# A long convolution as two blocks of 1024 with 1024-point transforms, in place of one 2048-point transform, beside a Fourier-mixing matmul

## The chip, the core and the metric

The kernel runs on one core of a Trainium2 chip. The metric is the device time of one execution in microseconds. Before the change the median of three runs is 596.75 us (596.72 to 599.88).

## What is computed

Two independent results are joined side by side. Part A multiplies a 2048 x 512 input by Fourier matrices on both sides and keeps the real part. Part B is a convolution of 2048 samples in each of 512 channels. Its kernel K is first built from 128 complex exponentials per channel.

```python
a = jnp.einsum("bsd,ed->bse", x, dft_hid_re)
b = jnp.einsum("bsd,ed->bse", x, dft_hid_im)
yA = jnp.einsum("ts,bse->bte", dft_seq_re, a) - jnp.einsum("ts,bse->bte", dft_seq_im, b)
...
K = 2.0 * jnp.einsum("dn,dnl->dl", C, P).real     # P = exp(A dt * position)
y = jnp.fft.irfft(jnp.fft.rfft(u_t, L2) * jnp.fft.rfft(K, L2)[None], L2)[:, :, :L]   # L2 = 2 L = 4096
yB = y.transpose(0, 2, 1) + u * D_skip
```

## The kernel before, in words

**The order of the work** is fixed when the program is built. A planner (`Plan`, line 71) runs every piece of work as a generator that names the engine it needs and an assumed duration. `run` (line 129) always takes the piece that can start first, and among equals the one with the lowest urgency number. The instructions of each engine come out in that order, and on the chip each engine follows its list strictly and waits where an operand isn't there. All DMAs but two are issued by one queue, SP.

**Part A** (class `Fnet`) is the filler. Its matmuls, line 299, have the highest urgency number, 5, so they go wherever TensorE has nothing else. There are 1920 of them, three for each product of a 128 x 128 by a 128 x 512 block. For them ScalarE and VectorE split each fp32 block that moves through the array into two halves, "hi" (line 184) and "lo" (line 186). One split serves twelve matmuls, and at most three splits are held ahead. The first stage's result goes to DRAM and is read back (lines 318 and 270). The last results leave by line 321.

**Part B** (class `Ssm`) goes through these steps.

- The input's first transform stage, `stage1_u` (line 788): 8 steps, each with matmuls (line 798), four evictions (line 808) and two stores to `xu` in DRAM (line 814).
- The tables of exponentials, in 16 chunks of 32 channels: `seed_args` and `seeds` (lines 560 to 606), `tables1` (line 640) and `tables2` (line 660). They are mostly VectorE work on lines 529, 538, 552 and 558, with squares on ScalarE (line 545). `tables2` has one buffer, so that a chunk's table can be started only when the previous one has been used.
- `taps` (line 707): 16 times 64 small matmuls (line 725), which turn a chunk's tables into samples of K. Two chunks make a group, for which `stage1_k` (line 743) does the kernel's first transform stage (line 755), and stores it to `xk` (line 769).
- The products, by four channel quarters h and four frequency groups q (`product`, line 865). Both spectra are loaded (line 849), the second transform stage runs on TensorE (line 876, 64 matmuls), ScalarE copies it out of PSUM (line 889), VectorE multiplies (lines 892, 894, 902, 905), TensorE does the first inverse stage (line 912), ScalarE copies it out (line 927), and it goes to `zs` in DRAM (line 933). Quarter h can start when its two kernel groups are stored, so the products of quarters 0 to 2 fall into the time of the tables and those of quarter 3 come after the last taps.
- The last inverse stage (`inverse`, line 948): `zs` is read back (line 954), 16 matmuls for each half quarter (line 959), and the output leaves by lines 975, 978 and 964 to 971.

Two PSUM buffers, f0 and f1, serve all of part B (`banks`, line 401). VectorE and ScalarE take part in both A and B.

The before form of the convolution is one transform of 2048 points at the frequencies k + 1/4, whose real part gives the 2048 wanted samples. A product is therefore one complex multiplication per frequency.

## Time and profile before

| What | Value |
|---|---|
| Median of three runs | 596.75 us |
| The profiled execution | 596.03 us |
| Its span, first to last instruction | 594.2 us |
| TensorE busy | 583.7 us (98%) |
| VectorE busy | 496.2 us (84%) |
| ScalarE busy | 380.7 us (64%) |
| DMA, mean | 212 GB/s, 125.97 MB |

The profile's page lists busy time per engine, the span in 40 slices, the chain of work that ended last, and groups of instructions by line. PE is TensorE, DVE VectorE, ACT ScalarE, SP the engine that issues the DMAs. A group's mean duration includes the time in which an instruction overlaps its neighbour, so the sum over a group can be larger than the engine's busy time. The timeline gives starts, from which the real spacing is read. 1.8 us of the execution lie outside the span.

### The profile page before, as it was taken

The page shows a single profiled execution, that of the slowest core. Times are in us where ns is not written, and L with a number is a line of the kernel's source. Part 1 is how long each engine was busy: PE and PEld are TensorE (multiplying, and loading weights), DVE is VectorE, ACT ScalarE, POOL GpSimd, SP SyncE. Part 2 cuts the span into 40 slices and gives each one's busy share as a digit, 9 for nine tenths or more (in the row PEclk, how much of TensorE's full clock was granted, in tenths as well). Part 3 has the DMA queues.
Part 4 walks back from the last instruction along what each step waited for, and adds up shares of the span by engine and source line. Part 5 has one row for each costly group of instructions (what it writes and reads, how often), then busy time and mean ns, then how long its engine had stood idle before and what let it go on. Part 6 is the DMA issues. An engine that isn't in the chain of part 4 may idle for free.

```text
span 594.2 us, 16953 instructions
## 1 busy us (share of the span) xinstructions
PE 583.7 (98%) x6982; PEld 451.0 (76%) x6982; DVE 496.2 (84%) x883; ACT 380.7 (64%) x745; POOL 4.7 (1%) x12
## 2 busy tenths in 40 slices
PE   7999999999999999999899999999999999999997
PEld 5866668778788777877687788778877877887775
DVE  6985989999999999999999999999999954255410
ACT  4689984856676767758574976677764635264532
POOL 0000000000000000000000000000000000000000
PEclk8999999999999999999999999999999999999999
DMA  8999996263394268546857793459798734998674
GB/s 270 295 334 362 310 362 202 77 208 94 98 267 126 90 183 252 144 136 157 251 179 207 200 256 131 140 154 278 234 276 225 241 114 145 287 358 258 186 248 143
DMA packets 141150, 125.97 MB, mean 212 GB/s; under 512 B 46224, under 2 KB 106128, under 8 KB 140816
## 3 DMA queue, kind: packets, MB, share of 16 engines
q1 hardware_dynamic: 140656, 124.49, 68.8%
q8 instruction: 55, 0.90, 0.6%
q10 hardware_dynamic: 416, 0.39, 0.2%
q14 instruction: 23, 0.19, 0.1%
HBM read 82.12 MB, written 42.73 MB: 210 GB/s over the span
## 4 chain that ended last, share of the span: by engine, by line
PE 82%; DVE 7%; ACT 6%; issue 2%; DMA 2%; SPq 0%; ACTq 0%; DVEq 0%
PE acc L299 64%; PE f L876 5%; PE f L725 5%; PE f L912 3%; PE f L959 3%; DVE prod L529 2%; PE f L755 2%; DVE lo L186 2%; DVE t L538 2%; ACT hi L184 1%; DMA uk<-in_x 1%; ACT L586 1%; DMA raw<-in_sT 1%; DMA xu<-z 1%; ACT seed L574 1%
## 5 line engine op out<-in xcount | busy, mean ns | idle before, releaser
L299 PE MATMUL acc<-hi,x_hi 128*128 128x512 f32 x640 | 257.8, 403 | 2.9 <-ACT x_hi L184 1.5
L299 PE MATMUL acc<-lo,x_hi 128*128 128x512 f32 x640 | 250.5, 391 | 0.1
L299 PE MATMUL acc<-hi,x_lo 128*128 128x512 f32 x640 | 250.4, 391 | 0.1
L529 DVE TENSOR_TENSOR prod<-t,cs 128x1024 f32<-128x1024 f32 (+4 forms) x192 | 163.3, 869 | 3.6 <-ACT t L667 1.4
L186 DVE TENSOR_TENSOR lo<-raw,hi 128x512 fp32r<-128x512 f32 x160 | 109.1, 686 | 63.9 <-ACT hi L184 63.9
L184 ACT ACTIVATE hi<-raw 128x512 fp32r<-128x512 f32 x160 | 100.3, 629 | 92.7 <-PE acc L299 72.8
L299 PEld LDWEIGHTS acc<-hi,x_hi 128*128 128x128 f32 x640 | 120.6, 188 | 48.4 <-issue 20.5
L299 PEld LDWEIGHTS acc<-hi,x_lo 128*128 128x128 f32 x640 | 120.6, 188 | 26.5 <-DVE x_lo L186 0.5
L299 PEld LDWEIGHTS acc<-lo,x_hi 128*128 128x128 f32 x640 | 120.7, 189 | 24.0 <-DVE lo L186 0.9
L538 DVE TENSOR_TENSOR t<-prod 128x512 f32<-128x512 f32 (+4 forms) x192 | 94.4, 511 | 1.1
L545 ACT ACTIVATE square<-t 128x256 f32<-128x256 f32 (+1 forms) x64 | 36.6, 572 | 22.9 <-DVE t L538 21.2
L313 ACT ACTIVATE y<-acc 128x512 f32<-128x512 f32 x48 | 28.4, 596 | 14.7 <-PE acc L299 12.8
L889 ACT ACTIVATE uk<-f 128x1024 f32<-128x1024 f32 x32 | 32.1, 1016 | 6.3 <-PE f L876 5.1
L725 PEld LDWEIGHTS f<-t,t 128*32 128x32 f32 x2048 | 29.5, 110 | 7.0 <-issue 4.3
L725 PE MATMUL f<-t,t 128*32 128x64 f32 x2048 | 32.2, 220 | 0.8 <-issue 0.8
L892 DVE TENSOR_TENSOR z<-uk 128x512 f32<-128x512 f32 x32 | 21.9, 686 | 8.4 <-ACT uk L889 7.6
L558 DVE TENSOR_TENSOR t<-square 128x128 f32<-128x128 f32 (+1 forms) x64 | 24.6, 384 | 0.3 <-ACT square L545 0.3
L927 ACT ACTIVATE z<-f 128x512 f32<-128x512 f32 x32 | 17.6, 596 | 10.9 <-PE f L725 5.8
L876 PE MATMUL f<-xt_k,w 64*32 64x128 f32 x1024 | 22.8, 271 | 1.0 <-issue 1.0
L604 ACT ACTIVATE cs<-cs 128x352 f32<-128x352 f32 x32 | 15.9, 537 | 12.1 <-DVE cs L599 12.1
L894 DVE TENSOR_TENSOR uk<-uk 128x512 f32<-128x512 f32 x32 | 22.1, 689 | 0.8
L552 DVE SCALAR_TENSOR_TENSOR t<-t 128x128 f32<-128x128 f32 (+2 forms) x48 | 22.3, 465 | 0.4
(85 smaller groups left out, 440.6 us busy)
## 6 DMA issues: line engine op xcount, KB each, us to landing
raw<-in_sT SPq DMA_DIRECT2D x127, 256.0 KB, 3.4
p<-y SPq DMA_DIRECT2D x32, 256.0 KB, 4.1
xt_u<-xu SPq DMA_DIRECT2D x32, 256.0 KB, 4.4
xk<-xk_sb SPq DMA_DIRECT2D x32, 256.0 KB, 4.0
xt_k<-xk SPq DMA_DIRECT2D x32, 256.0 KB, 5.1
zs<-z SPq DMA_DIRECT2D x32, 256.0 KB, 3.7
zl<-zs SPq DMA_DIRECT2D x16, 512.0 KB, 6.1
raw<-p SPq DMA_DIRECT2D x32, 256.0 KB, 3.8
```

Of the source, the lines that this page charges most:

```text
L184: self.nc.scalar.activation(hi, src, AF.Copy)
L186: self.nc.vector.tensor_tensor(lo, src, hi.bitcast(F32), op=OP.subtract)
L299: nc.tensor.matmul(acc[d], l[:, cols], r, start=k == 0 and n == 0, stop=k == len(items) - 1 and n == 2)
L313: self.nc.scalar.activation(y, ps, AF.Copy, scale=-1.0 if g[2] == 1 else 1.0)
L529: self.nc.vector.tensor_tensor(p.rearrange("p k d c m -> p k (d c) m"), src.rearrange("p d c l -> p (d c) l")[:, None, :, rows].to_broadca ...
L538: self.nc.vector.tensor_tensor(dst[:, :, :, rows], p[:, 0], p[:, 1, :, ::-1], op=OP.add)
L545: self.nc.scalar.activation(sq, t[:, :, :, m // 2:m], AF.Square)
L552: self.nc.vector.scalar_tensor_tensor(t[:, :, 1, m:2 * m:2], t[:, :, 0, m // 2:m], 2.0, t[:, :, 1, m // 2:m], op0=OP.mult, op1=OP.mult)
L558: self.nc.vector.tensor_tensor(t[:, :, 0, m:2 * m:2], box[0][:, :, 0], box[0][:, :, 1], op=OP.subtract)
L725: nc.tensor.matmul(ps[32 * j:32 * j + 32, i], t1[:, d, c], t2[:, d, c], start=c == 0, stop=c == 1, tile_position=(0, 32 * j))
L876: nc.tensor.matmul(got[r][1][32 * xx:32 * xx + 32, g, o:o + PART], self.w2[rows, 2 * q + r, xx, 32 * c:32 * c + 32], xt[rows, r, xx], star ...
L889: a.activation(uk[:, r].rearrange("p g n c d -> p g (n c d)"), p, AF.Copy)
```

## The change

The 2048 samples are cut into two blocks of 1024, and the transforms have 1024 points, at k + 1/4. From the blocks U0, U1 of the input and K0, K1' of the kernel (the first kernel stage's constants add K0 times i to the second block) come two spectra: U0 K0 for the first output block, and U0 K1' + U1 K0 for the second. That is three complex multiplications for two output frequencies, where there were two. The data volume of the spectra stays the same.

- First stages: `f1u` has 32 rows and 64 columns per tile in place of 64 and 128. A step of `stage1_u` has eight matmuls of 512 columns in eight positions of the array, where it had four in two positions.
- Second stage: the same 64 matmuls per product, with the blocks on the two halves of the partitions. The spectra's loads and the stores to `zs` now cover 64 partitions each (two per group, one for each block), where each covered 128.
- The product has ten VectorE operations of 128 x 512 where it had six.
- Last inverse stage: 32 matmuls in eight positions for each half quarter, where there were 16 in two positions. The last quarter is fetched back from `zs` by groups, in eight DMAs of 16 partitions with 16 KB on each, and is evicted by ScalarE and VectorE in two steps at the end. Before, it came in four pieces of 128 partitions.
- Buffers: quarter 3's four input spectra are loaded early, into the buffers of quarters 0 to 2, and its kernel spectra have four buffers. The product has three in the last phase.
- Planner: ScalarE's seeds, squares and table copies get a more urgent number (`URGENT`), an event of the first split is set earlier, and the product waits for the last kernel group.

The core of the diff:

```diff
+URGENT = (lambda: -0.5),
...
-        yield "pe", 1.82
-        for m in range(2):
-            for r in range(2):
-                rows = slice(64 * r, 64 * r + 64)
-                nc.tensor.matmul(got[m][1][:, r], self.f1u[rows], u[rows, m], start=True, stop=True,
-                                 tile_position=(64 * r, 0))
+        yield "pe", 0.95
+        for r in range(4):
+            for h in range(2):
+                rows = slice(32 * r, 32 * r + 32)
+                nc.tensor.matmul(got[r // 2][1][64 * h:64 * h + 64, r % 2], self.f1u[rows], u[rows, h], start=True,
+                                 stop=True, tile_position=(32 * r, 64 * h))
...
-        for r in range(2):
-            self.nc.sync.dma_start(xt[:, r], view[2 * q + r])
+        for g in range(2):
+            self.nc.sync.dma_start(xt[64 * g:64 * g + 64].rearrange("p r x d -> p (r x) d"), view[g, q])
...
-            v.tensor_tensor(P[:, r], t[:, r], u[:, r], op=OP.mult)
-            yield "dve", dve(512), *APART
-            v.tensor_tensor(t[:, r], t[:, r], u[:, r, :, ::-1], op=OP.mult)
...
+            v.tensor_tensor(P[:, r], t[:, r], u[:, r, 0:1].to_broadcast([128, 2, 2, PART]), op=OP.mult)
+        yield "dve", dve(512), *APART
+        v.tensor_tensor(W, t[:, :, 0], u[:, :, 1], op=OP.mult)
+        yield "dve", dve(512)
+        v.tensor_tensor(P[:, :, 1], P[:, :, 1], W, op=OP.add)
+        yield "dve", dve(512), *APART
+        v.tensor_tensor(W, t[:, :, 0], u[:, :, 1, ::-1], op=OP.mult)
+        for r in range(2):
+            yield "dve", dve(512), *APART
+            v.tensor_tensor(t[:, r], t[:, r], u[:, r, 0:1, ::-1].to_broadcast([128, 2, 2, PART]), op=OP.mult)
...
         v.tensor_tensor(u[:, :, :, 0], P[:, :, :, 0], P[:, :, :, 1], op=OP.subtract)
         self.plan.put(b.zbs)
         yield "dve", dve(512), *APART
+        v.tensor_tensor(t[:, :, 1], t[:, :, 1], W, op=OP.add)
+        yield "dve", dve(512)
         v.tensor_tensor(t[:, :, :, 0], t[:, :, :, 0], t[:, :, :, 1], op=OP.add)
...
+    def fetch_last(self, z, q, left):
+        yield "dma", load(512), *URGENT
+        for g in range(2):
+            self.nc.sync.dma_start(z[64 * g + 16 * q:64 * g + 16 * q + 16],
+                                   self.zs[3][g, 8 * q:8 * q + 8].rearrange("s c l d -> (s c) l d"))
...
-        yield "pe", 0.1 + 0.1025 * n
-        for w in range(n // 2):
-            for y in range(2):
-                nc.tensor.matmul(ps[64 * y:64 * y + 64, w // 4, PART * (w % 4):PART * (w % 4) + PART],
-                                 self.ib[:, n * i + 2 * w + y], z[:, 2 * w + y], start=True, stop=True,
-                                 tile_position=(0, 64 * y))
+        yield "pe", 0.95
+        for w in range(m):
+            for j in range(4):
+                for g in range(2):
+                    rows, l = slice(64 * g, 64 * g + 64), 4 * w + j
+                    nc.tensor.matmul(ps[32 * j:32 * j + 32, g, PART * w:PART * w + PART], self.ib[rows, n * i + l],
+                                     z[rows, l], start=True, stop=True, tile_position=(64 * g, 32 * j))
...
+        if h == 3:
+            yield "act", act(512)
+            nc.scalar.activation(*part(0), AF.Copy)
+            yield "dve", dve(512)
+            nc.vector.tensor_copy(*part(1))
+            self.give(k)
+            for g, queue in enumerate((nc.sync, nc.scalar if i else nc.sync)):
+                queue.dma_start(y[:, g], part(g)[0])
```

## The prediction

> **What bounds the kernel now.** I read the busy shares first, then the stages, the chain, the groups of instructions and the timeline. The page's slices:

> ```profile
> PE   7999999999999999999899999999999999999997
> ...
> DVE  6985989999999999999999999999999954255410
> ACT  4689984856676767758574976677764635264532
> ```

> TensorE is full from end to end. VectorE is just as full until the last table is done at 481.7 us, and half idle afterwards. The stages, cut at the first matmuls and at that moment (columns: start:end, length, then busy us of PE, PEld, DVE, ACT, POOL; clock, DMA share, GB/s), and two pieces of interest:

> ```profile
> 8.25:481.69 473.44, 470.77 (x5533) 365.04 (x5534) 454.68 (x817) 327.93 (x662) 4.28 (x7) 1.00 0.69 209
> 481.69:594.20 112.51, 107.80 (x1439) 83.11 (x1437) 37.99 (x57) 48.05 (x77) 0.24 (x1) 0.99 0.73 223
> ...
> 40.00:52.00 12.00, 12.00 (x52) 7.98 (x52) 3.62 (x7) 11.89 (x26) 0.00 (x0) 1.00 0.98 351
> ...
> 500.00:550.00 50.00, 50.00 (x702) 39.14 (x701) 21.25 (x32) 23.51 (x38) 0.00 (x0) 1.00 0.95 284
> ```

> So two engines bound the first 482 us together, and TensorE alone the rest. The chain (start, length, piece) shows TensorE's pieces and, at the end, its cover:

> ```profile
> 482.09 1.05 PE f L912 x32
> 483.14 1.90 PE f L725 x122
> ...
> 548.33 1.05 PE f L912 x32
> ...
> 554.97 1.96 PE f L876 x128
> ...
> 563.29 1.05 PE f L912 x32
> 564.34 12.47 PE acc L299 x54
> 576.81 1.02 PE f L959 x16
> ...
> 580.65 1.90 PE f L959 x32
> 582.55 7.76 PE acc L299 x33
> ```

> The reader is to see the length of each kind of burst, and that 54 matmuls of part A (12.5 us) stand between the last L912 and the first L959 that needs its result. A run of n L299 costs 0.2266 n + 0.25 us (x12 2.97, x102 23.36 in the same chain).

> **TensorE's work.** A first-stage step is 1.92 us (L798 x8), eight of them. The new one has 16 executions of 512 columns in eight array positions; L912 has 32 of 256 in eight positions of the same 32*64 shape, as many columns, and takes 1.05. Saved: 8 x 0.87 = 7.0. A half quarter of the last stage is 1.90 (L959 x32); the new one has half the columns of L876 (1.96, eight positions of 64*32), so 0.98. Saved: 8 x 0.92 = 7.4. Part B interrupts L299 60 times, not 62: 0.5. If TensorE alone counted, the span would be 594.2 - 14.9 = 579.3. If the positions didn't overlap the gain is 0 at worst; neither row leaves room for much under half.

> **VectorE's work.** A product has ten operations for six. L892 to L905 are 0.60 us apart where the next doesn't need the last one's result, 0.73 where it does; the mean sum of the six is 3.85. Broadcast operands cost nothing (L529 with them 685 ns at 512 columns, L892 686). Ten with three or four dependent neighbours: 10 x 0.60 + 3.5 x 0.12 = 6.4. Added: 2.6 a product, 41 us in all. On average 496 + 41 fits into 579. It doesn't fit where it falls: in the compiled order, 11 of the 16 products stand ahead of the last table.

> **When the last taps (L725) can start.** The order of the instructions gives what stands ahead of them.
> - TensorE: 1725 L299 in place of 1587 (+138 x 0.2266 = 31.3), one more second stage (1.96), two more interruptions (0.5), less 7.0 for the first stage and four half quarters (3.7): 483.1 + 23.1 = 506.2.
> - VectorE: 11 x 2.6 = 28.6 and 11 more splits at 0.60 (6.6): 483.1 + 35.2 = 518.3.

> VectorE is the later one. But it was idle before 130 us for 17.5 us, of which 8.4 lie in 40 to 52, where ScalarE was full (row above) with seeds, table loads and evictions of the first stage. In the new order the first-stage steps come further apart (after 96, 135, 183 matmuls of part A; before after 102, 120, 135), and seeds are more urgent. I take those 8.4 as recovered: 518.3 - 8.4, **510**. Ends: 506.2 and 518.3. VectorE waiting means that TensorE waits at the next taps, since its order is fixed.

> **From there to the end.** Before: 594.2 - 483.1 = 111.1. Off go 138 L299 (31.3), the second stage (1.96), four half quarters (3.7) and four interruptions (1.0): 73.1. Then comes a new wait. After the last L912 only 27 L299 are left (6.4 us), then the last L959. Between them lie eviction, store to zs and fetch. Before, L912 ended at 564.34, the fetch was issued at 570.33 (6.0), and fetches landed after 5.6 us: 11.6 in all, hidden under 12.5. Now 11.6 - 6.4 = 5.2 us are bare (ends 3.5 and 8). Nothing is queued behind the waiting L959 but the end. It ends with an eviction and an output DMA (out_yb 2.6 us to landing, out_ya 2.3) with one more eviction in series (at most 0.69): 0.7 later than before (3.9).

> 510 + 73.1 + 5.2 + 0.7 = 589.0 span; the execution has 1.8 us outside it (596.03 - 594.2): **591**. The median of 596.75 lies 0.7 above the profiled execution; half a per cent of it, about what this measurement can tell from no change, is 593.8 to 599.7.

> TensorE's clock: the first L299 ran at 0.246 us each (x97 in 23.90), later 0.2266; an idle of 2 us near 290 left it at 1.00. [...]

> **Costed at nothing:** ScalarE's new priorities and early loads of quarter 3's input spectra (ScalarE is 64% busy, and the early loads lie where DMA's share is 0.63, between 103 and 482); smaller constants. If the early loads were late they would cost TensorE a product's loading, about 5 us.

> **Rivals.**
> 1. *VectorE recovers more* (the tables keep up with TensorE): 506.2, so 587. Against it: 11 products' additions come into a stretch with 1% idle.
> 2. *VectorE recovers nothing*: 518.3, so 599. For it: ScalarE's number of instructions is unchanged (749 to 747), so its backlog may only move.
> 3. *The SP queue becomes the bound of the tail* (slower). After the last kernel group (about 6 us after the last taps) the order has 67 transfers' worth of 256 KB, 17.6 MB. At 500 to 550 us a share of 0.95 moved 284 GB/s, so one costs 0.88 us of the queue and all 59, in 73 us: 14 us of slack. 30 of them now touch only 64 or 16 partitions (8 spectrum loads of the kernel and 4 of the input, 10 stores, 8 fetches). No row shows such a transfer. Between "as a wide one" (0) and "twice" (30 x 0.88 = 26 more) I take 0 for the forecast, the nearest rows being wide ones of the same bytes; it decides from 1.5 times on. At twice: 26 - 14 = 12 us, 603. They queue in one line, so the late fetches pay.
> 4. *The array positions don't overlap as in L912 and L876*: 14.4 more, 605. Against it: same shapes in both rows.

> [...]

> **Chances.** Forecast (510, wide-like transfers) 0.37; rival 1 0.10; rival 2 0.17; rival 3 0.32; rival 4 0.04. The forecast's own range is 587 to 596 (its waits' ends); rival 3 from 595 (half the price) to 605. Eight in ten: from below rival 1, where the bare wait is at its short end, to rival 3: 584 to 604. Faster by over 0.5%: most of the forecast and rival 1, 0.44. Within: rival 2 and the edges, 0.21. Slower: rivals 3 and 4 and a late rival 2, 0.35.

> **What would show it.** First-stage steps of 1.05 and half quarters of about 1.0 us in the chain; products of ten operations, 6.4 us where nothing stands between; the last L725 at 510 (506 rival 1, 518 rival 2), with idle of TensorE ahead of taps; a bare wait of 5 us before the last L959, ended by the fetch from zs. Rival 3: landings of the 64-partition loads and of the fetches well above 5 us, with the DMA share near 1 and L876 or the first L959 waiting for them. I would be wrong if ScalarE, not VectorE, holds the tables, or if evictions that wait for stores stop ScalarE's queue.

## The result, and the profile after

The changed kernel takes 619.86 us (median of six executions, 615.0 to 622.4), the kernel before 596.9 us beside it. The ratio is 1.0363, 95% interval 1.0311 to 1.0415: slower by 3.6%, where 591 us and a range of 584 to 604 had been forecast. The profiled execution takes 622.4 us with a span of 620.6. All executions compared below are undisturbed ones; one of the four of `after_zuk` was in a slower state of the chip and is left out of its median.

The slices of the page after:

```profile
PE   8999999999999989999999998999879999979772
...
DVE  6999989999999998999997998989979999256700
...
PEclk9999999999999999999999999999899999999895
```

TensorE, full to the end before, has a small gap near 220 us, more of them from 370 us on and a thin end. VectorE is full until the last table, which is done at 520.3 us instead of 481.7. The granted clock, at 9 tenths or more before in all slices but the first, has dents at 434 to 450 us, at 574 to 590 and at the end. The same by stages, cut at the last taps, with two pieces of 10 us (columns: start:end, length, busy us of PE, PEld, DVE, ACT, POOL; clock, DMA share, GB/s):

```profile
8.25:521.46 513.21, 499.09 (x6028) 387.31 (x6030) 488.34 (x874) 343.51 (x683) 3.54 (x7) 0.99 0.73 202
521.46:620.60 99.14, 75.15 (x1267) 55.56 (x1267) 42.95 (x67) 33.75 (x53) 0.52 (x1) 0.90 0.88 203
440.00:450.00 10.00, 7.59 (x86) 5.56 (x86) 8.75 (x16) 4.42 (x8) 0.00 (x0) 0.83 0.72 269
550.00:560.00 10.00, 7.22 (x144) 5.45 (x143) 6.72 (x11) 3.65 (x5) 0.00 (x0) 0.83 1.16 238
```

In the last stage the DMA share rises from 0.73 to 0.88 while the rate falls from 223 to 203 GB/s: the engines are busier and move less. TensorE is idle for 24 us of 99. The chain (start, length, piece) names what for:

```profile
457.68 1.92 PE f L735 x126
459.60 3.67 issue
...
521.46 1.93 PE f L735 x128
...
540.15 6.50 DMA xt_k<-xk
...
552.03 2.78 issue
...
574.81 11.76 DMA zl<-zs
...
602.48 9.20 DMA zl<-zs
611.81 3.72 PE f L1018 x126
```

Three things stand here that the chain of before didn't have: loads of spectra and fetches of `zs` for which TensorE waits, "issue" waits of up to 3.67 us in the middle of a burst of matmuls (0.80 in the chain of before), and last matmuls that take 3.72 us where 128 at the full clock take 2.2 (64 take 1.09). The DMA issues of the page (count, KB each, median us from issue to landing) answer to 5.1 for `xt_k` and 3.7 for `zs` before:

```profile
xt_k<-xk SPq DMA_DIRECT2D x32, 256.0 KB, 7.2
zs<-z SPq DMA_DIRECT2D x32, 256.0 KB, 4.4
```

### The profile page after: what moved, and what is told of

Its sections match the earlier page's. It is cut to its first block, busy times and chain, and to the rows that moved or that the text cites. A ratio compares the mean times of both kernels' runs of the same rounds, so it can differ in the third digit from the quotient of the medians.

```text
span 620.6 us, 17639 instructions
## 1 busy us (share of the span) xinstructions
PE 580.5 (94%) x7302; PEld 446.6 (72%) x7302; DVE 534.8 (86%) x948; ACT 381.8 (62%) x743; POOL 4.3 (1%) x12
## 4 chain that ended last, share of the span: by engine, by line
PE 51%; DVE 25%; DMA 12%; issue 6%; ACT 4%; SPq 1%; ACTq 0%; DVEq 0%
PE acc L307 39%; DVE prod L538 7%; DMA zl<-zs 5%; DVE lo L194 5%; DVE t L547 4%; PE f L735 4%; PE f L902 3%; DMA par<-par_dram 2%; DMA xt_k<-xk 2%; PE f L947 2%; PE f L810 1%; PE f L1018 1%; PE f L765 1%; DVE z L924 1%; DMA raw<-in_wT 1%
## 5 line engine op out<-in xcount | busy, mean ns | idle before, releaser
L321 ACT ACTIVATE y<-acc 128x512 f32<-128x512 f32 x48 | 28.6, 596 | 23.2 <-PE acc L307 14.7
L913 ACT ACTIVATE uk<-f 128x1024 f32<-128x1024 f32 x32 | 31.9, 1020 | 12.5 <-PE f L902 12.5
L902 PE MATMUL f<-xt_k,w 64*32 64x128 f32 x1088 | 24.8, 275 | 4.6 <-issue 3.5
L1018 PE MATMUL f<-zl,ib 64*32 64x128 f32 x512 | 12.6, 327 | 15.6 <-DMA zl<-zs 15.6
L962 ACT ACTIVATE z<-f 128x512 f32<-128x512 f32 x32 | 17.5, 588 | 9.5 <-PE f L947 7.2
L1018 PEld LDWEIGHTS f<-zl,ib 64*32 64x32 f32 x512 | 9.1, 125 | 19.5 <-issue 15.7
```

What stands on the lines that cost most here:

```text
L321: self.nc.scalar.activation(y, ps, AF.Copy, scale=-1.0 if g[2] == 1 else 1.0)
L902: nc.tensor.matmul(got[r][1][32 * xx:32 * xx + 32, g, o:o + PART], self.w2[rows, 8 * q + 4 * r + xx, 32 * c:32 * c + 32], xt[rows, r, xx], ...
L913: a.activation(uk[:, r].rearrange("p g n c d -> p g (n c d)"), p, AF.Copy)
L1018: nc.tensor.matmul(ps[32 * j:32 * j + 32, g, PART * w:PART * w + PART], self.ib[rows, n * i + l], z[rows, l], start=True, stop=True, tile_ ...
```

## The experiments

Three theories stood at the start. *Transfers*: loads, stores and fetches that touch 64 or 16 partitions take longer in the one line of the SP queue. *Tables*: VectorE's 44 more operations ahead of the last table hold the taps. *Order*: the new priorities (on ScalarE's work and on a few loads) give a worse order. A fourth, of the instruction blocks, came up on the way.

### Each cause alone, in the kernel before

`before_narrow`: spectra loaded and `zs` stored as two transfers of 64 partitions in place of two of 128, the same bytes.

```diff
-        for r in range(2):
-            self.nc.sync.dma_start(xt[:, r], view[2 * q + r])
+        for g in range(2):
+            self.nc.sync.dma_start(xt[64 * g:64 * g + 64].rearrange("p r x d -> p (r x) d"), view[q, g])
```

> The kernel before, with the spectra's loads and the stores to zs done as two transfers of 64 partitions in place of two of 128: the same bytes and rows of 512 bytes, 96 transfers, and the order of every engine unchanged. Narrow theory (64 partitions are slower to reach than 128): the loads of the kernel's spectra land in about 7 us, not 5, and the kernel is 3 to 10 us slower, most of it after 500 us where the queue was at a share of 0.95. Tables theory (the added VectorE operations alone hold up the table stage): no difference, within 1.5 us.

`before_ten`: four more operations of 128 x 512 in each product, planned anew.

```diff
+        for x in (P[:, 0], t[:, 0], P[:, 1], t[:, 1]):
+            yield "dve", dve(512), *APART
+            v.tensor_tensor(x, x, x, op=OP.max)
```

> The kernel before, with four more VectorE operations of 128 x 512 in each product (each takes the larger of a value and itself, so nothing changes), planned as the others are. TensorE's work and the transfers are those of before. Tables theory: the last taps move from 483 to about 515 and the time rises by 5 to 15 us, because part A's filler is used up by then. Narrow theory: TensorE stays full, the table stage just takes more of the filler, within 3 us of before.

`before_narrow` takes 614.3 us, ratio 1.0286 (1.0221 to 1.0352); `before_ten` 616.9 us, ratio 1.0339 (1.0305 to 1.0373). Either alone is enough for most of the loss, and both cost more than their theories had expected (3 to 10 us, 5 to 15). The last taps start at 490.5 us in the first and at 516.9 in the second. The first shows its cause in the piece from 500 to 550 us, which before moved 284 GB/s under a TensorE without a gap:

```profile
500.00:550.00 50.00, 44.82 (x475) 34.12 (x474) 16.84 (x25) 21.58 (x34) 0.00 (x0) 0.93 0.92 228
```

The share is nearly as high (0.92 for 0.95), and a fifth less gets through. In its DMA issues the landings of `xt_k` go from 5.1 us to 6.4, by the width alone:

```profile
xt_k<-xk SPq DMA_DIRECT2D x32, 256.0 KB, 6.4
```

In the second, TensorE hardly waits ahead of the last taps. The plan, made anew for ten operations, has put 1728 of part A's matmuls (L299) ahead of them where there were 1587, and that much cover is missing behind them. TensorE's two longest waits (what for, us in total, times, longest) both lie there:

```profile
PE f L962 <- DMA zl<-zs: 8.8, 1, 8.8
PE f L915 <- DVE uk L905: 3.9, 1, 3.9
```

### One part taken back, in the changed kernel

`after_six` leaves out the four added VectorE operations (the second block lacks the product U1 K0); the order is otherwise the same.

```diff
-        v.tensor_tensor(W, t[:, :, 0], u[:, :, 1], op=OP.mult)
-        v.tensor_tensor(P[:, :, 1], P[:, :, 1], W, op=OP.add)
-        v.tensor_tensor(W, t[:, :, 0], u[:, :, 1, ::-1], op=OP.mult)
-        v.tensor_tensor(t[:, :, 1], t[:, :, 1], W, op=OP.add)
```

> The changed kernel without the four added VectorE operations of each product (the second block lacks U1 K0), the order of everything else unchanged. Tables theory: the last taps start at 506 to 510 in place of 521, the time falls by 10 to 15 us. Narrow theory: it falls by 3 us at most, since the waits after the last taps are for transfers.

`after_wide` fetches the last quarter in four transfers of 128 partitions, once all of it is stored.

```diff
+        for o in range(16 * i, 16 * i + 16, 8):
+            self.nc.sync.dma_start(z[:, o:o + 8], self.zs[3].rearrange("b s c l d -> (b s c) l d")[:, o:o + 8])
```

> The changed kernel with the last quarter fetched from zs in four transfers of 128 partitions, when all of it is stored, in place of eight of 16 partitions by groups; all engines but the SP queue keep their order. Narrow theory: the last wait of TensorE falls from 14 us to 5 to 8, the clock stays up in the last stage, the time falls by 7 to 11 us. Tables theory: no difference beyond 2 us.

615.0 us, ratio 1.0313 (1.0277 to 1.0349), and 613.0 us, ratio 1.0301 (1.0237 to 1.0366). Executed in this order, the operations are worth 5 us at most and move the last taps by 3 (518.2): VectorE isn't what the taps wait for. The run keeps the plan for ten operations, though, with its 1725 matmuls of part A ahead of the last taps, so what the operations cost through the plan it can't show. A fetch that starts later but is wide is worth about as much (6.9 us), and leaves the taps where they were (520.0).

### Order, or width

`after_plain` has the old priorities throughout.

```diff
-URGENT = (lambda: -0.5),
+URGENT = ()
```

> The changed kernel with no task of the plan marked urgent, so that the order is planned anew by due times alone; the transfers, the matmuls and VectorE's ten operations a product are the same. Theory of the order (the urgent tasks fill ScalarE's line with work that is not due, and the tables' evictions stand behind it): the last taps move from 521 to 510 or below and the time falls by 10 us or more, to some 610. Theory of the transfers (narrow ones take longer in one line): the last taps stay within 4 us of 521 and the time within 5 us of 620. Theory of the tables (VectorE's 44 more operations ahead of the last table): the same as the transfers' theory, as VectorE has as much ahead of the last table in either order.

`after_uk` loads the spectra of kernel and input by 128 partitions too, by another layout in DRAM; the input's stores of the first stage become narrow for it.

```diff
-        self.xu = dram.tile([2, 32, 2, 32, DM], F32, name="xu")
+        self.xu = dram.tile([32, 2, 2, 32, DM], F32, name="xu")
...
-            self.nc.sync.dma_start(xt[64 * g:64 * g + 64].rearrange("p r x d -> p (r x) d"), view[g, q])
+            self.nc.sync.dma_start(xt[:, g], view[2 * q + g])
```

> The changed kernel with the kernel's spectra, the input's spectra and the last quarter's fetch loaded by transfers of 128 partitions and the same bytes; the input's spectra are therefore stored, in the first stage, in twice as many transfers of 64 partitions and half the bytes. The stores to zs stay narrow. The order on TensorE, VectorE and ScalarE is unchanged. Theory of the transfers: the loads of the kernel's spectra land after 5.1 us instead of 7.2, the last taps move from 521 towards 512, the time falls 12 to 17 us, to about 605. Theory of the tables: the last taps stay at 518 to 521, and only the waits of the last 100 us go, 7 to 9 us as with the wide fetch alone: 611 to 613.

`after_kwide` does so for the kernel's spectra alone.

> The changed kernel with the wide fetch and the kernel's spectra loaded by transfers of 128 partitions; the input's spectra are loaded by 64 and stored wide, as in the changed kernel. Theory of the transfers, each with its share: after the wide fetch 613, with the input's spectra wide too 603; 32 transfers of the kernel and 26 of the input carry the ten us between them, so 606 to 609. If the kernel's loads alone were what counted (the longest landings, 7.2 us): 603 to 605. If only the input's: 611 to 613.

`after_zuk` makes the stores to `zs` wide as well, and its fetches narrow with long rows.

```diff
-        for g in range(2):
-            nc.sync.dma_start(view[g, q], z[64 * g:64 * g + 64].rearrange("p r x d -> p (r x) d"))
+        for r in range(2):
+            nc.sync.dma_start(view[2 * q + r], z[:, r])
...
+        for g in range(2):
+            self.nc.sync.dma_start(z[64 * g:64 * g + 64], self.zs[h][:, g, :, 16 * i:16 * i + 16])
```

> As the one before, and the stores to zs are 128 partitions wide as well; the fetches of zs become transfers of 64 partitions with rows of 8 KB instead of 128 partitions with rows of 4 KB. Theory of the transfers by partitions alone: little is gained over the one before, as narrow fetches take the place of narrow stores (within 4 us). If it is the short rows of narrow transfers (512 B) that cost and not the partitions, the long rows make it 3 to 6 us faster than the one before. Theory of the tables: within 2 us of the one before.

`after_uk_six` is `after_uk` without the four operations.

> The changed kernel with the loads of after_uk and without the four added operations of the product (the second block lacks the product of its own spectrum with the kernel's first), the order otherwise the same. Theory of the tables: the last taps come at 506 to 510, by TensorE's own work, and the time is near 596. Theory of the transfers: the last taps are within 4 us of those of after_uk, as the wide loads alone have already brought them there. If neither is enough, and ScalarE's line holds the tables, the last taps stay above 514 in both.

| Kernel | median us | ratio to before (95%) | last taps |
|---|---|---|---|
| after_plain | 627.4 | 1.0527 (1.0453 to 1.0602) | 537.1 |
| after_kwide | 608.4 | 1.0194 (1.0154 to 1.0235) | 522.0 |
| after_uk | 603.2 | 1.0118 (1.0045 to 1.019) | 513.8 |
| after_zuk | 611.3 | 1.0223 (1.0144 to 1.0301) | – |
| after_uk_six | 601.7 | 1.0079 (1.0055 to 1.0103) | 515.2 |

Order is out: without the priorities the time is worse by 7 us, which no theory had expected, and not better. The tables as they are executed are nearly out: with wide loads, all 64 operations of the four cost 1.5 us, within the two intervals. What they cost through the plan, `after_uk_six` shows no more than `after_six` (its last taps, expected at 506 to 510 by the tables' theory, start at 515.2); that part isn't excluded for the 6 to 7 us by which `after_uk` is still slower than before. Width carries the greater part: 16.7 us of 23 between the changed kernel and `after_uk`, in which TensorE, VectorE and ScalarE have the same instructions in the same order. Its landings (the same view as above) are back at, or near, the values of before (5.1 and 3.7), those of `zs` although its stores are still narrow:

```profile
xt_k<-xk SPq DMA_DIRECT2D x32, 256.0 KB, 5.3
zs<-z SPq DMA_DIRECT2D x32, 256.0 KB, 3.7
```

Its stages, cut at the last taps as in the changed kernel above:

```profile
8.25:513.77 505.52, 496.77 (x6024) 386.57 (x6022) 487.60 (x874) 343.01 (x683) 3.40 (x7) 1.00 0.70 205
513.77:600.28 86.51, 71.73 (x1268) 52.70 (x1267) 42.38 (x66) 33.55 (x54) 0.24 (x1) 0.92 0.83 232
```

The last stage moves 232 GB/s at a share of 0.83, where the changed kernel moves 203 at 0.88. TensorE's idle time (the length less PE's busy time) falls from 14.1 to 8.8 us ahead of the last taps and from 24.0 to 14.8 behind them.

`after_zuk` is a miss: I had expected it level or better for its rows of 8 KB. Its narrow fetches, for which TensorE waits at the end, seem to cost more than narrow stores (the two intervals overlap a little), and long rows don't make up for it.

### The prices by themselves

`probe` runs streams of twelve transfers of 256 KB, and after them bursts of matmuls with and without transfers. The bursts are there for a row of the DMA list, 57 packets of 16 KB in a queue named "instruction", in the changed kernel:

```profile
q8 instruction: 57, 0.93, 0.7%
```

> Nothing of the computation: streams of transfers of 256 KB, twelve each, on the SP queue, parted by a VectorE operation; then three times 45 matmuls of 512 columns with 128 of the taps' matmuls behind them, first without transfers, then under 40 wide ones, under 40 narrow ones, and without again. Theory of the transfers: one of 128 partitions costs 0.8 to 0.9 us of the stream, one of 64 partitions 1.1 to 1.5, in alternating halves as in one half alone, one of 16 partitions 2 us or more; long rows (4 KB) of 64 partitions are no better than rows of 512 B; stores like loads. If instead each narrow transfer costs as much as a wide one (0.9), the loss of the change has another cause. On the taps: TensorE's instructions are fetched in blocks of 16 KB by the same DMA engines, and if such a block comes late behind data, the taps under transfers hold waits of 1 to 4 us that nothing in the profile ends, while those without transfers hold none or shorter ones; if the waits come from something else, all four parts look alike.

The streams in order: 128 partitions in rows of 2 KB, the same in rows of 512 B, 64 partitions in alternating halves (512 B), 64 in the lower half alone (512 B), 64 alternating with rows of 4 KB, 16 partitions with 16 KB each; then stores, of 128 and of 64 alternating (512 B). A mixed stream before the stores is left out, as its transfers waited for one another. Columns as in the stages above; TensorE's bursts lie beside the first four:

```profile
14.45:27.26 12.81, 10.57 (x279) 9.12 (x278) 0.00 (x0) 0.00 (x0) 0.00 (x0) 0.87 0.73 248
27.48:41.28 13.80, 12.68 (x296) 10.62 (x295) 0.00 (x1) 0.00 (x0) 0.00 (x0) 1.00 0.85 232
41.50:58.98 17.48, 12.66 (x290) 10.65 (x289) 0.00 (x1) 0.00 (x0) 0.00 (x0) 0.85 0.94 182
59.19:78.76 19.57, 10.26 (x43) 8.08 (x41) 0.00 (x1) 0.00 (x0) 0.00 (x0) 0.85 1.02 161
78.97:95.22 16.25, 0.00 (x0) 0.00 (x0) 0.00 (x1) 0.00 (x0) 0.00 (x0) 0.50 0.84 194
95.43:123.87 28.44, 0.00 (x0) 0.00 (x0) 0.01 (x2) 0.00 (x0) 0.00 (x0) 0.50 0.91 111
148.02:160.58 12.56, 0.00 (x0) 0.00 (x0) 0.00 (x1) 0.00 (x0) 0.00 (x0) 0.50 0.88 251
160.79:176.28 15.49, 0.00 (x0) 0.00 (x0) 0.00 (x1) 0.00 (x0) 0.00 (x0) 0.50 0.81 203
```

A twelfth of the differences is the price of one: 0.31 us more for 64 partitions in alternating halves (17.48 - 13.80), 0.48 in one half alone, 0.29 with rows of 4 KB against 2 KB rows of 128, 0.24 for a store, and 1.30 for 16 partitions (28.44 - 12.81). The reader is to see the two last columns together: a narrow stream keeps the DMA share as high and moves less. In two longer streams of 40, both beside bursts, 260 GB/s for wide ones and 187 for narrow ones make 1.01 and 1.40 us each.

Against wide streams of the same rows, 64 partitions move 0.69 of the rate in one half alone (161 against 232) and 0.72 to 0.78 in alternating halves (187 against 260, 182 against 232); 16 partitions come to 111 GB/s. Twelve transfers took 17.48 us in alternating halves and 19.57 in one half, a tenth more.

### TensorE's clock

In the changed kernel's trace half the clock is granted from 607.0 us on, within TensorE's last long wait (8.5 us, from 601.7). `after_uk_awake`: seven matmuls that nothing uses, ahead of the last wait.

```diff
+        if h == 3 and not i:
+            for _ in range(7):
+                nc.tensor.matmul(ps[:, 0], self.ib[:, :4].rearrange("p a b -> p (a b)"),
+                                 self.ib[:, :16].rearrange("p a b -> p (a b)"), start=True, stop=True)
```

> The changed kernel with the wide loads of after_uk, and seven matmuls that nothing uses ahead of the last wait of TensorE (6.6 us), 0.85 us each, so that TensorE is at work while it would wait. If the granted clock halves after an idle window, as the records say, the last 128 matmuls run in 1.1 us for 64 instead of 2.2, and the end comes 1.5 to 2 us sooner: about 601.5. If the longer time of these matmuls comes from the data's arrival, nothing changes: 603.

The end of TensorE's timeline (start, length, instructions, idle before), in `after_uk` and then here:

```profile
590.04 1.11 PE L1025 MATMUL f<-zl,ib 64*32 64x128 f32 x32 [6.57 <-DMA zl<-zs]
...
593.24 2.29 PE L1025 MATMUL f<-zl,ib 64*32 64x128 f32 x64 [0.69 <-ACT zl L1031]
```

```profile
596.81 0.67 PE L1029 MATMUL f<-zl,ib 64*32 64x128 f32 x32 [0.71 <-DMA zl<-zs]
598.12 0.67 PE L1029 MATMUL f<-zl,ib 64*32 64x128 f32 x32 [0.64 <-DMA zl<-zs]
600.10 0.67 PE L1029 MATMUL f<-zl,ib 64*32 64x128 f32 x32 [1.31 <-DMA zl<-zs]
601.28 1.03 PE L1029 MATMUL f<-zl,ib 64*32 64x128 f32 x32 [0.51 <-DMA zl<-zs]
```

32 matmuls take 0.67 us instead of 1.11, so the longer time was the clock's doing; the last 32 take 1.03, and from 601.5 us on the trace again grants half the clock. The end doesn't come sooner (604.6 us, ratio 1.0166, 1.0126 to 1.0206): each piece now waits for its own landing. The expected 1.5 to 2 us are a miss.

### TensorE's instructions

TensorE's waits in `after_uk` (line, what for, us in total, times, longest) still hold one that no data explains, in the middle of the taps of 450 us:

```profile
PE f L736 <- issue: 4.7, 3, 3.4
```

While it lasts, VectorE waits for ScalarE, ScalarE for the taps, and the taps, with 4 of 128 matmuls left, for nothing shown. I counted TensorE's records in the trace. In the changed kernel the "issue" waits stand at the records 7105, 7873, 8641, 10433, 12993 and 13249; all of them leave 193 when divided by 256. So do those of over 0.6 us in every other run, the kernel before and `probe` included, but for four of 0.65 to 1.08 us (one of them, of 0.75 us, in the changed kernel), all at the same place of the program: the first matmuls on `xt_k` in a second stage (540 to 546 us), where the record itself names a semaphore to wait for. The DMA list has a queue of instructions with packets of 16 KB, and 57 of them for the changed kernel's 14,677 records of TensorE, 55 for the 14,053 before: 256 records a packet. At the wait above, one such packet arrives among the data (the DMA queues from 453 to 454 us, in `after_uk`):

```profile
q1 hardware_dynamic: 192, 0.38, 97.0%
q8 instruction: 1, 0.02, 5.7%
```

It ends at 454.1 us, and TensorE goes on at 455.5. At the longest wait of the changed kernel and at the four longest of `probe` under the two long streams the packet likewise ends 1.3 to 1.6 us before TensorE goes on. The taps use 256 instructions in 1.9 us; the reading is that where a block ends inside a dense stretch, the next one has 2 to 4 us to come through engines that are full (the share of the data in the row above is 97.0%). `probe` shows what the transfers do to it: after 45 large matmuls, 256 small ones (two blocks), under wide transfers, under narrow ones, and without:

```profile
211.60 3.15 PE L147 MATMUL pt<-zero 128*32 128x64 f32 x209
217.46 1.42 PE L147 MATMUL pt<-zero 128*32 128x64 f32 x47 [2.71 <-issue]
```

```profile
250.66 3.66 PE L147 MATMUL pt<-zero 128*32 128x64 f32 x247
257.80 0.33 PE L147 MATMUL pt<-zero 128*32 128x64 f32 x9 [3.48 <-issue]
```

```profile
301.12 3.56 PE L147 MATMUL pt<-zero 128*32 128x64 f32 x240
305.95 0.43 PE L147 MATMUL pt<-zero 128*32 128x64 f32 x16 [1.28 <-issue]
```

Without transfers the waits are 0.9 to 1.3 us (three bursts), under wide ones 0.9 to 2.7, under narrow ones 1.2 to 4.4. At most of the 57 block boundaries of the changed kernel no such wait of over 0.6 us stands; at six, those above, TensorE waited 0.6 to 3.7 us.

`after_uk_shift` moves the count by 128, `after_shift` does so in the changed kernel as it is.

```diff
-        for n in range(3):
-            self.nc.tensor.matmul(ps[:, :256], z[:, :128], z[:, 256:], start=n == 0, stop=n == 2)
+        for n in range(2):
+            self.nc.tensor.matmul(ps[:, :256], z[:, :128], z[:, 256:], start=n == 0, stop=n == 1)
+        for n in range(33):
+            self.nc.tensor.matmul(ps[:32, :64], z[:, :32], z[:, 256:320], start=True, stop=True,
+                                  tile_position=(0, 0))
```

> The changed kernel with the wide loads of after_uk and 128 more instructions of TensorE ahead of all others: one of the three matmuls that only warm the array up is left out and 33 small ones (32 columns by 64) are put in, whose results nothing uses. In every run so far the waits of TensorE that nothing in the profile ends stand at the same place of its own count of instructions, 193 beyond a multiple of 256, and where the 256 before had gone in 2 to 4 us. Theory of the blocks (instructions come in blocks of 256 by the DMA engines, and one that follows a quickly used one comes late): the wait of 3.4 us in the taps of 452 us goes, and shorter or equal ones come where the shifted count has such a pair: near 204, 231, 259, 424, 488 and 510 us; all still at 193 beyond a multiple of 256. Theory of the data (the taps of 452 wait for their tables): the wait stays at these taps. The time is within 4 us of 603 either way.

> The changed kernel with nothing but the shift of TensorE's count of instructions by 128 (one warming matmul left out, 33 small ones put in). If the late blocks are a loss of their own beside the narrow transfers, the waits of 3.7 us in the taps of 460 us and of 2.8 us at 552 go, with their half-clock windows, and the time falls by 4 to 7 us, to 613 to 616. If the transfers alone set the pace, the tables and loads are as late as before, other waits take the place of these, and the time stays within 2 us of 620.

`after_uk_shift` takes 600.1 us, ratio 1.0062 (1.004 to 1.0085), 3 us less than `after_uk`, though the two intervals overlap; the last taps start at 510.8 instead of 513.8. The wait in the taps of 450 us is gone, and the ones that are left, none over 1 us, stand at other places of the program and again at 193. `after_shift` takes 615.1 us, ratio 1.0292 (1.0247 to 1.0337): 5 us less, at intervals that just overlap, as expected of a loss of its own, though one wait of 3 us only moved to another burst.

### The end of the line

`after_uk_last` is `after_uk_shift` with part A's four last output stores held back behind the last fetch.

```diff
+        if g == ("p", 3, None):
+            yield self.hold
         yield "dma", load(256)
```

> The changed kernel with wide loads and the shift of after_uk_shift, and part A's last four output stores held back until the last fetch from zs is issued; the orders of TensorE and VectorE are the same, and ScalarE's last eviction for part A comes later. If these 1 MB in the line ahead of the fetch make it late, its landing falls from 8.8 us to 5.6 to 6.5, TensorE's wait ahead of it from 7.9 to 5 or 6, and the time by 2 to 3 us, to 597 to 598, level with the kernel before. If eviction, store and fetch take that long by themselves, the wait stays and the time is 600.

598.45 us, ratio 1.0028 (1.0006 to 1.0051). The last pieces of the chain, in `after_uk_shift` and then here:

```profile
582.02 8.79 DMA zl<-zs
590.85 1.19 PE f L1028 x32
```

```profile
581.33 4.94 DMA zl<-zs
586.31 1.19 PE f L1032 x32
```

The fetch lands after 4.9 us instead of 8.8, TensorE's wait before it falls from 7.9 to 4.1, and the changed kernel is within 0.3% of the one before. The step from `after_uk_shift`, 1.7 us, is within the two intervals. None of the versions beats the kernel before.

## Why the prediction was wrong

**The step that failed** is the price of the narrow transfers: "Between 'as a wide one' (0) and 'twice' [...] I take 0 for the forecast, the nearest rows being wide ones of the same bytes". One of 64 partitions costs 0.3 to 0.4 us more, one of 16 costs 1.3. By these, the 22 and 8 of the tail come to about 18 us (22 x 0.35 + 8 x 1.3), where 14 us of slack stood against them: 4 us by the prediction's own reckoning. Making the loads and the last fetch wide gave back 16.7 us. Rival 3 named the cause, and its "twice" (26 us for the 30, 12 beyond the slack, 603) lay nearer to the measured time than the forecast's nothing, partly by luck: its 0.88 us more for each is over twice the measured price of 64 partitions and two thirds of that of 16. No run shows the addition that leads to the 605 at the upper end of its range; the measured prices put the 18 us above in its place, which end at 595. The rival was also too mild in its form. It asked when the line would be full, but TensorE waits for single loads and fetches long before that (`xt_k` 7.2 us from issue to landing), and more than a third of what the wide loads gave back (7.7 of 20.3 us of span) lies ahead of the last taps, where I had counted no narrow transfer and the DMA share over the whole stage is 0.73: 521.5 us against 513.8.

Point by point:

- *TensorE's bursts*: right. The chain has the first-stage step at 1.05 us; the half quarter takes 1.09 to 1.11 where 0.98 was forecast. Rival 4 is out.
- *VectorE's work*: right. Busy time rises by 38.6 us (496.2 to 534.8), 41 forecast.
- *The last taps at 510*: near for the kernel with wide loads (513.8, and 510.8 with the count shifted too), but by luck. The prediction took VectorE for the later engine, 518.3 less 8.4 recovered. In none of the changed kernel's versions in this order does TensorE wait for a table ahead of the last taps, and without the added operations they start at 515.2 (`after_uk_six`). What sets them is TensorE itself, as in rival 1: its 506.2 and what it idles and loses at half clock beyond before give 519 for the changed kernel and 512 for `after_uk`, within 2 us of the measured 521.4 and 513.8. The time of 518 in rival 2 nearly came true, but not for its reason.
- *The bare wait of 5.2 us (ends 3.5 and 8)*: right with the transfers mended. It is 8.5 us in the changed kernel, with the narrow fetch and 1 MB of output stores in the line ahead of it; and 4.1 with both taken away.
- *The clock*: the forecast counts no time for it. 126 of the last matmuls take 3.72 us, and the trace has four more stretches of 3.41 us at half clock, near 443, 464, 556 and 587 us. They stand behind waits that add up to 2.0 to 3.1 us in the 3.41 us before. At most 1.7 us, half of its length, are lost in each stretch. Before had such a stretch too, from 8.9 to 12.3 us, among the first 97 L299, which the prediction read as 0.246 us each. The 2 us near 290 us that left its clock at 1.00 were two waits, 1.18 us in one step of 3.41 us and 1.05 in the next.
- *ScalarE's priorities at nothing*: all the urgent marks together, those of a few loads included, are worth 7 us.
- *Not in the sum*: instruction blocks. "issue" waits of TensorE go from 3.0 to 11.3 us (0.75 of them not at a block boundary), and two of the half-clock stretches follow them.

From the forecast to the measurement, each upon the last (medians; the runs are of several series, and the steps carry some 3 us of uncertainty each): 591 forecast; 598.5 with everything below taken back; 600.1 with the output stores in their old place; 603.2 with the blocks as they fell; 608.4 with the input's spectra narrow; 613.0 with the kernel's too; 619.9 with the fetch of 16 partitions. What is left of 7.5 us between 591 and 598.5 is partly seen (the half clock at the end, the bare wait, instruction waits of 2.4 us): 3 us lie ahead of the last taps (513.0 in that profile) and 5 behind them. The rest stays open. The causes alone, in the kernel before, cost 17 us (transfers) and 20 (operations, with the plan made anew). Less the 14 to 15 us that the change saves TensorE by the prediction's count, which the bursts bear out, they come to 22 or 23, the measured loss; and 20 less 14 is about what `after_uk` still loses. That is an estimate from sums of separate runs: no run has the changed kernel planned anew for six operations, which would test it.

## What to carry to other kernels

A layout that puts two blocks on the two halves of the partitions pays for it at each transfer (0.24 to 0.48 us for 256 KB in `probe`): keep the transfer at 128 partitions by the layout in DRAM, and look at GB/s beside the DMA share, since a narrow stream looks just as busy (in `probe` a share of 0.94 at 182 GB/s, where a wide one had 0.85 at 232). Where no row shows a transfer's form, a forecast should price it by its partitions and by who waits for its landing, not by its bytes. An "issue" wait in the middle of a dense burst of matmuls is worth counting out modulo 256 (all but four of those over 0.6 us stood at 193 in these runs). And a run that leaves work out but keeps the planned order tests only the execution: what the work did to the plan is still in it.
